# Key and strided-query loads in rows of 2 KB, and the first 64 tokens of all heads sorted by four ScalarE copies

## The chip, the core and the metric

The kernel runs on one core of a Trainium2 chip. Its time is the device time of one execution in microseconds (us); lower is better. TensorE (PE) does matmuls and transposes, VectorE (DVE), ScalarE (ACT) and GpSimd (POOL) do the elementwise work, and SyncE (SP) issues nearly every transfer, in the order of the program. 16 DMA engines move the data.

## The reference

The first half is attention with two kinds of heads over 8 batches, 8 heads, 576 tokens and 64 dimensions, and the second half is a soft mixture of experts over its output.

```python
scores = scale * np.matmul(q, k.transpose(0, 1, 3, 2))
rel = pos[:, None] - pos[None, :]
mask_local = (rel >= 0) & (rel < stride)                       # stride = 32
mask_strided = (rel >= 0) & (pos[None, :] % stride == pos[:, None] % stride)
masks = np.stack([mask_local if h < H // 2 else mask_strided for h in range(H)])
...                                   # softmax over the last axis, times v
x = attn_out.transpose(0, 2, 1, 3).reshape(B * S, H * D)       # 4608 x 512
logits = x @ phi                                               # 512 x 32
...                    # softmax over the tokens: d; softmax over the slots: c
slot_input = d.T @ x                                           # 8 experts x 4 slots
h = np.maximum(slot_input[e] @ w1[e], 0.0); slot_out[e] = h @ w2[e]
return c @ slot_out
```

So a token of a local head looks at the 32 last tokens, and one of a strided head at every 32nd token before it. Everything is in float32.

## The kernel before, in words

The attention runs in 16 steps, numbered i. Step i takes two local heads (called L) and two strided heads (called S) of batch i // 2. For tokens 64 to 575 it loads four arrays of 256 KB, `kL`, `qL`, `kS`, `qS` (`emit_D`, one transfer each, L306). For the first 64 tokens an even step loads a fifth array `t` with all eight heads of k and q, in two transfers of 128 KB (`emit_Dt`, L311). Values come in other transfers (L316 and L319 for local heads, L324 for strided heads, where each transfer has 36 rows of 4 KB), and between all of them a written-out list places loads of the experts' weights, 512 KB each (`w` in the list, L256).

In a load of L306 each of 128 partitions gets, for each of two heads, four consecutive tokens of 64 dimensions, so the memory is read in pieces of 1 KB. In the load of L311 each partition is one token, and the memory is read in pieces of 256 B, one for each head.

TensorE turns each loaded array over by four transposes of 128x128 into a bank of PSUM (`turn`, L340). ScalarE then copies the bank to SBUF and sorts it on the way: `kL` by four copies of 64 partitions by 256 elements (L356), `qL`, `qS` and `t` by one copy of 128 by 512 each (L350, L360, L375), `kS` by two copies (L364). From the copy of `t` (called `et`, into the last third of the tile `qtb`) GpSimd takes the keys of the first 64 tokens into the key tiles (`emit_kc`: L383, L387). Then come the scores (`emit_SL`, `emit_SS`, L390), a softmax on VectorE and ScalarE, and the products with the values (L470).

The order of all this work on every engine is set by one list that is written out by hand, `ORDER`. A name in it is a part and a step: `DkL.0` is the load of `kL` for step 0, `Tt.0` the transposes of `t`, `et.0` its copy. Each engine executes its instructions in the order of the list. The loads of one step go into a ring of four places in the tile `natb`, so a load also waits until an older one has been transposed.

After step 15 the sums over all tokens are merged, the first expert layer runs (L851), then the second (L963), and the results are combined and stored (L988, L996, L1010 to L1028).

Of the kernel before, what the change touches and what calls it, by code (L numbers as in the profile page):

```python
# [19 lines left out]
B, H, S, D = 8, 8, 576, 64  # L20
# [6 lines left out]
NI = 36  # L27
# [81 lines left out]
def tile_sparse_attention_soft_moe(  # L109
# [12 lines left out]
    nc = tc.nc  # L122
    P = 128
    ACT, DVE, PC = nc.scalar.copy, nc.vector.tensor_copy, nc.gpsimd.tensor_copy
# [6 lines left out]
    def big(nm, cols, dt=F32):  # L131
        return const.tile([P, cols], dt, name=nm)
# [10 lines left out]
    d = big("d", 128)  # L143
# [6 lines left out]
    kLb, kSb = big("kLb", 2 * S), big("kSb", 2 * S)  # L150
    qtb = big("qtb", 1536)
# [16 lines left out]
    def nat(x, i):  # L168
        if (x, i) in EARLY:
            lo = 512 * EARLY[x, i]  # L170
            return xnb[:, lo:lo + 512]
        lo = 512 * (USES.index((x, i)) % 4)
        return natb[:, lo:lo + 512]
# [6 lines left out]

    kL = kLb.rearrange("p (a t) -> p a t", a=2)
    kt = {"kL": kLb, "kS": kSb, "qL": qtb[:, 0:512], "qS": qtb[:, 512:1024]}
    tl = qtb[:, 1024:1536].rearrange("p (j x t) -> p j x t", j=4, x=2)

    psg = {1: pb[:, 0:640].rearrange("p (s k a) -> p s k a", s=5, a=2),
           2: pb[:, 640:1152].rearrange("p (s x) -> p s x", s=4)[:, :, 0:3 * NI].rearrange("p s (k a) -> p s k a", a=3)[:, :, :, 0:2]}
# [30 lines left out]
    def take():  # L217
        x = min(freed, key=lambda x: freed[x])
        del freed[x]
        return banks[x], x  # L220

    def give(t):
        clock[0] += 1
        freed[t[1]] = clock[0]
# [75 lines left out]
    def heads(i, s):  # L300
        h = 2 * (i % 2) + (4 if s == "S" else 0)
        return slice(h, h + 2)

    def emit_D(x, i):
        src = (k if x[0] == "k" else q)[i // 2, heads(i, x[1]), 64:]
        nc.sync.dma_start(out=nat(x, i).rearrange("p (h x) -> p h x", h=2), in_=src.rearrange("h (p n) d -> p h (n d)", n=TN))  # L306

    def emit_Dt(i):

        for x, src in enumerate((k, q)):  # L310
            nc.sync.dma_start(out=nat("t", i)[x::2].rearrange("t (h d) -> t h d", d=D), in_=src[i // 2, :, 0:64].rearrange("h t d -> t h d"))  # L311

    def emit_Dv(i):

# [32 lines left out]
    def emit_e(x, i):  # L347
        t = box.pop(("T" + x, i))
        if x == "qL":
            ACT(out=kt[x].rearrange("d (p n) -> d p n", n=TN), in_=t[0].rearrange("d (n p) -> d p n", n=TN))  # L350
        elif x == "kL":

            for a in range(2):
                dst = kL[64 * a:64 * a + 64, a, 64:]
                for n in range(2):
                    ACT(out=dst.rearrange("d (p j n) -> d p j n", j=2, n=2)[:, :, :, n],  # L356
                        in_=t[0][64 * n:64 * n + 64].rearrange("d (h j p) -> d p j h", j=2, h=2)[:, :, :, a])
        elif x == "qS":

            ACT(out=kt[x].rearrange("d (x m i) -> d x m i", m=4, i=32), in_=t[0].rearrange("d (x i m) -> d x m i", i=32, m=4))  # L360
        else:
            for n in range(2):
                r = slice(64 * n, 64 * n + 64)
                ACT(out=kt[x][r].rearrange("d (x m n i) -> d x m n i", m=4, n=2, i=NI)[:, :, :, n, 4:],  # L364
                    in_=t[0][r].rearrange("d (x i m) -> d x m i", i=32, m=4))
        give(t)
# [5 lines left out]

    def emit_et(i):
        t = box.pop(("Tt", i))
        ACT(out=tl, in_=t[0].rearrange("d (j t x) -> d j x t", j=4, x=2))  # L375
        give(t)

    def emit_kc(s, i):

        for a in range(2):  # L380
            h = slice(64 * a, 64 * a + 64)
            src = tl[h, i % 2 + (2 if s == "S" else 0), 0]
            PC(out=kL[h, a, 0:64] if s == "L" else kA[h, a], in_=src)  # L383
            if s == "S":
                for n in range(2):
                    dst = kSb[64 * n:64 * n + 64].rearrange("d (h j m x) -> d h j m x", h=2, m=4, x=2 * NI)[:, a, :, :, NI * n:NI * n + 4]
                    PC(out=dst, in_=src.rearrange("d (i m j n) -> d j m i n", i=4, m=4, n=2)[:, :, :, :, n])  # L387

    def score(t, c, x, wd, lhsT, rhs):
        nc.tensor.matmul(out=t[0][32 * c:32 * c + 32, x:x + wd], lhsT=lhsT, rhs=rhs, start=True, stop=True, skip_group_check=True)  # L390
# [8 lines left out]
    def emit_SS(i):  # L399
        t = box["M2", i] = take()  # L400
        for c in range(4):
            qa = tl[:, i % 2 + 2 * (c // 2), 1, 32 * (c % 2):32 * (c % 2) + 32]
            score(t, c, 0, 128, qa, kL[:, :, 0:64] if c < 2 else kA)
        for h in range(2):
            for z in range(2):
                for c in range(4):

                    x = 8 * h + 4 * z + c
                    score(t, c, 128 + 2 * NI * (2 * h + z), 2 * NI, kt["qS"][:, 32 * x:32 * x + 32], kSb[:, 2 * NI * x:2 * NI * x + 2 * NI])

    def part(t, which):
# [286 lines left out]
    for x in KQ:  # L698
        fns["D" + x] = lambda i, x=x: emit_D(x, i)
        fns["T" + x] = lambda i, x=x: emit_T(x, i)  # L700
        fns["e" + x] = lambda i, x=x: emit_e(x, i)
# [6 lines left out]
    for s in "LS":  # L708
        fns["kc" + s] = lambda i, s=s: emit_kc(s, i)
        fns["P" + s] = lambda i, s=s: emit_P(s, i)  # L710
        fns["f" + s] = lambda i, s=s: emit_f(s, i)
        fns["n" + s] = lambda i, s=s: emit_n(s, i)
        fns["X" + s] = lambda i, s=s: emit_X(s, i)
    fns.update(Dt=emit_Dt, Tt=emit_Tt, et=emit_et, Dv=emit_Dv, Ds=emit_Ds, C2=emit_C2, SL=emit_SL, SS=emit_SS, rc=emit_rc, PA=emit_PA,
               fA=emit_fA, AL=emit_AL, AS=emit_AS, AA=emit_AA, nA=emit_nA, xL=emit_xL, xS=emit_xS,
               XB=emit_XB, xB=emit_xB, LG=emit_LG, lc=emit_lc, lg=emit_lg, T9=emit_T9, x9=emit_x9, G9=emit_G9, c9=emit_c9, b9=emit_b9,
# [200 lines left out]
    for x in ORDER:  # L917
# [4 lines left out]
        else:  # L922
            n, i = x.split(".")
            i = int(i)
# [147 lines left out]
```

## Time and profile before

| | |
|---|---|
| median of 3 runs | 243.8 us (243.25 to 244.0) |
| the profiled execution, its own time | 242.59 us |
| its span from the first to the last instruction | 240.8 us |
| TensorE busy | 215.2 us, 89% of the span |
| VectorE busy | 165.6 us, 69% |
| ScalarE busy | 154.3 us, 64% |
| GpSimd busy | 86.0 us, 36% |
| moved by DMA | 72.73 MB, mean 302 GB/s |

The profiled execution took 1.8 us more than its span, and 1.2 us less than the median of the runs. A busy time is the time in which at least one instruction of the engine was under way; TensorE's matmuls overlap one another, so its share says little on how much more it could do. The share of DMA is the mean over 16 engines and can be a little over 1, since packets of one engine overlap.

### The profile page before, as it was taken

To read this page: it belongs to the slowest core of one execution; us is meant where nothing else is said; L and a number is where in the kernel's file an instruction comes from. 1 tells how busy PE (TensorE), PEld (TensorE's weight loads), DVE (VectorE), ACT (ScalarE), POOL (GpSimd) and SP (SyncE) were. 2 spreads that over 40 slices of the span, in tenths; PEclk is the share of its full clock that TensorE was granted. 3 is DMA by queue.
4 is the path that set the end of the run, shared out by engine and by line. 5 is a ranking of instruction groups with operands and counts; after the bars stand their busy time and mean duration, and the time that the engine had idled before them with its cause. 6 is when DMAs were issued, how large, how long until landed. Compare 5 with 4: busy or idle time off the path is not lost.

```text
span 240.8 us, 9926 instructions
## 1 busy us (share of the span) xinstructions
PE 215.2 (89%) x4096; PEld 169.0 (70%) x4096; DVE 165.6 (69%) x381; ACT 154.3 (64%) x347; POOL 86.0 (36%) x189
## 2 busy tenths in 40 slices
PE   8899998998889999999999999899889999998700
PEld 3688897888778998897889898687753246455400
DVE  6097997896599978887977786799872831145900
ACT  2789898786769889878697988666440241135700
POOL 5466835626443271743327434733102000000000
PEclk9999999999999999999999999999999999999975
DMA  5987999989997998899999899999998999887996
GB/s 151 351 231 238 301 282 279 302 207 318 304 321 218 299 317 236 263 344 297 318 367 340 233 280 335 316 284 358 349 344 338 395 377 312 293 287 257 381 399 260
DMA packets 69597, 72.73 MB, mean 302 GB/s; under 512 B 32896, under 2 KB 59664, under 8 KB 69552
## 3 DMA queue, kind: packets, MB, share of 16 engines
q1 hardware_dynamic: 69184, 71.84, 92.2%
q8 instruction: 32, 0.52, 0.9%
q0 software_dynamic: 80, 0.15, 0.2%
q10 hardware_dynamic: 288, 0.11, 0.2%
q14 instruction: 13, 0.11, 0.2%
HBM read 62.65 MB, written 9.44 MB: 299 GB/s over the span
## 4 chain that ended last, share of the span: by engine, by line
PE 54%; DMA 18%; DVE 13%; issue 4%; ACT 3%; POOL 2%; SPq 1%; DVEq 0%; POOLq 0%; ACTq 0%
PE bank L340 10%; PE bank L390 7%; PE bank L470 7%; DMA natb<-in_q_dram 6%; PE bank L851 6%; DMA vs<-in_v_dram 5%; PE bank L518 4%; DMA wb<-in_moe_w_dram 4%; PE bank L963 3%; PE bank L462 3%; PE bank L276 2%; PE bank L988 2%; DVE xnb L500 2%; DMA natb<-in_k_dram 2%; PE bank L549 2%
## 5 line engine op out<-in xcount | busy, mean ns | idle before, releaser
L340 PE MATMUL bank<-cf,natb 128*128 128x128 f32 x276 | 40.2, 277 | 3.0 <-DMA natb<-in_k_dram 1.3
L340 PEld LDWEIGHTS bank<-cf,natb 128*128 128x128 f32 x276 | 30.8, 141 | 8.0 <-issue 3.0
L356 ACT COPY kLb<-bank 64x256 f32<-64x256 f32 x64 | 25.8, 403 | 7.5 <-PE bank L340 4.7
L427 DVE TENSOR_TENSOR pb<-bank,cb 128x512 f32<-128x512 f32 (+2 forms) x48 | 21.7, 472 | 11.4 <-PE bank L390 7.4
L500 DVE TENSOR_TENSOR xnb<-bank,rz 128x512 f32<-128x512 f32 (+1 forms) x33 | 21.6, 669 | 7.6 <-PE bank L470 4.9
L330 POOL COPY vb<-vb 64x1024 f32<-64x1024 f32 x16 | 16.7, 1041 | 25.8 <-DMA vb<-in_v_dram 14.8
L390 PE MATMUL bank<-kLb,qtb 128*32 128x128 f32 x576 | 23.1, 274 | 0.8 <-POOL kLb L383 0.8
L442 DVE TENSOR_REDUCE rz<-pb 128x10 f32<-128x640 f32 (+1 forms) x32 | 21.6, 684 | 1.0 <-ACT pb L439 0.6
L466 ACT COPY ptb<-bank 128x512 f32<-128x512 f32 x32 | 19.0, 598 | 4.5 <-PE bank L462 2.9
L432 DVE TENSOR_REDUCE mx<-pb 128x10 f32<-128x640 f32 (+1 forms) x32 | 21.5, 685 | 0.5
L435 DVE TENSOR_TENSOR pb<-pb,mx 128x640 f32<-128x640 f32 (+1 forms) x32 | 21.1, 673 | 0.3
L439 ACT ACTIVATE pb<-pb 128x640 f32<-128x640 f32 (+1 forms) x32 | 18.6, 597 | 3.5 <-DVE pb L435 3.3
L335 POOL COPY natb<-natb 128x512 f32<-128x512 f32 x15 | 9.6, 638 | 30.1 <-DMA natb<-in_q_dram 18.9
L462 PE MATMUL bank<-cf,pb 128*128 128x128 f32 x128 | 19.4, 276 | 0.8 <-ACT d L619 0.7
L518 PE MATMUL bank<-cf,xnb 128*128 128x128 f32 x128 | 18.8, 277 | 0.7 <-DVE xnb L500 0.5
L390 PEld LDWEIGHTS bank<-kLb,qtb 128*32 128x32 f32 x576 | 17.1, 110 | 3.4 <-POOL kLb L383 1.5
L364 ACT COPY kSb<-bank 64x512 f32<-64x512 f32 x32 | 18.6, 581 | 0.4
L387 POOL COPY kSb<-qtb 64x32 f32<-64x32 f32 x64 | 17.5, 273 | 2.4
L470 PE MATMUL bank<-vs,ptb 128*32 128x128 f32 x480 | 16.0, 274 | 2.4 <-DMA vs<-in_v_dram 1.1
L470 PE MATMUL bank<-vb,ptb 128*32 128x128 f32 x512 | 17.4, 274 | 0.0
L331 POOL COPY vb<-vb 64x1024 f32<-64x1024 f32 x16 | 16.8, 1048 | 0.7
L518 PEld LDWEIGHTS bank<-cf,xnb 128*128 128x128 f32 x128 | 14.4, 141 | 2.6 <-issue 1.2
(199 smaller groups left out, 457.2 us busy)
## 6 DMA issues: line engine op xcount, KB each, us to landing
wb<-in_moe_w_dram SPq DMA_DIRECT2D x48, 512.0 KB
natb<-in_k_dram SPq DMA_DIRECT2D x30, 256.0 KB
natb<-in_q_dram SPq DMA_DIRECT2D x30, 256.0 KB
vb<-in_v_dram SPq DMA_DIRECT2D x32, 144.0 KB
vs<-in_v_dram SPq DMA_DIRECT2D x30, 144.0 KB
out_dram<-wb SPq DMA_DIRECT2D x16, 256.0 KB
vb<-in_moe_w_dram SPq DMA_DIRECT2D x4, 512.0 KB
xnb<-in_moe_w_dram SPq DMA_DIRECT2D x3, 512.0 KB
```

The source lines that it names most:

```text
L340: nc.tensor.transpose(out=t[0][:, 128 * n:128 * n + 128], in_=src[:, 128 * n:128 * n + 128], identity=ident)
L356: ACT(out=dst.rearrange("d (p j n) -> d p j n", j=2, n=2)[:, :, :, n], in_=t[0][64 * n:64 * n + 64].rearrange("d (h j p) -> d p j h", j=2, ...
L390: nc.tensor.matmul(out=t[0][32 * c:32 * c + 32, x:x + wd], lhsT=lhsT, rhs=rhs, start=True, stop=True, skip_group_check=True)
L427: nc.vector.tensor_tensor(out=dst, in0=src, in1=masks[w].unsqueeze(1).unsqueeze(3).to_broadcast([P, n, kk, 2]), op=ALU.add)
L432: nc.vector.tensor_reduce(out=part(box[i][0], w), in_=psg[w].rearrange("p s k a -> p s a k"), op=ALU.max, axis=AX.X)
L435: nc.vector.tensor_tensor(out=psg[w], in0=psg[w], in1=over(box[i][0], w), op=ALU.subtract)
L442: nc.vector.tensor_reduce(out=part(box[i][1], w), in_=psg[w].rearrange("p s k a -> p s a k"), op=ALU.add, axis=AX.X)
L462: nc.tensor.transpose(out=t[0][:, 128 * r:128 * r + 128], in_=pb[:, lo + 128 * r:lo + 128 * r + 128], identity=ident)
L466: ACT(out=ptL if s == "L" else ptS, in_=t[0])
L470: nc.tensor.matmul(out=t[0][32 * c:32 * c + 32, 128 * r:128 * r + 128], lhsT=lhsT, rhs=rhs, start=True, stop=True, skip_group_check=True)
L500: nc.vector.tensor_tensor(out=xn[:, place(i, s), r0:r0 + nr].rearrange("p r (a d) -> p r a d", a=2), in0=t[0][:, 128 * r0:128 * r0 + 128 * ...
L518: nc.tensor.transpose(out=t[0][:, 128 * r:128 * r + 128], in_=xn[:, place(i, s), r, :], identity=ident)
```

## The change

The loads of `kL`, `kS` and `qS` now give each partition eight consecutive tokens of one head, 2 KB in one piece. `qL` keeps its pieces of 1 KB. The load of `t` gives each of 64 partitions eight consecutive tokens of one head, again 2 KB in one piece, with k in partitions 0 to 63 and q in 64 to 127. After the transposes the tokens then stand in another order. For `kL` the four copies take another stride. For `t` the one copy of 128 by 512 becomes four copies of 64 by 256. The strided copies of GpSimd and the choice of columns in the strided scores follow the new order of tokens. `ORDER` stays as it is.

```diff
-    tl = qtb[:, 1024:1536].rearrange("p (j x t) -> p j x t", j=4, x=2)
+    tl = qtb[:, 1024:1536].rearrange("p (x j t) -> p j x t", j=4, x=2)
...
     def emit_D(x, i):
         src = (k if x[0] == "k" else q)[i // 2, heads(i, x[1]), 64:]
+        if x != "qL":
+            nc.sync.dma_start(out=nat(x, i), in_=src.rearrange("h (p n) d -> p h (n d)", n=8))
+            return
         nc.sync.dma_start(out=nat(x, i).rearrange("p (h x) -> p h x", h=2), in_=src.rearrange("h (p n) d -> p h (n d)", n=TN))
...
-            nc.sync.dma_start(out=nat("t", i)[x::2].rearrange("t (h d) -> t h d", d=D), in_=src[i // 2, :, 0:64].rearrange("h t d -> t h d"))
+            nc.sync.dma_start(out=nat("t", i)[64 * x:64 * x + 64], in_=src[i // 2, :, 0:64].rearrange("h (p n) d -> h p (n d)", n=8))
...
                 for n in range(2):
-                    ACT(out=dst.rearrange("d (p j n) -> d p j n", j=2, n=2)[:, :, :, n],
-                        in_=t[0][64 * n:64 * n + 64].rearrange("d (h j p) -> d p j h", j=2, h=2)[:, :, :, a])
+                    ACT(out=dst.rearrange("d (p b n) -> d p b n", b=4, n=2)[:, :, :, n],
+                        in_=t[0][64 * n:64 * n + 64].rearrange("d (b p h) -> d p b h", b=4, h=2)[:, :, :, a])
...
     def emit_et(i):
         t = box.pop(("Tt", i))
-        ACT(out=tl, in_=t[0].rearrange("d (j t x) -> d j x t", j=4, x=2))
+        for n in range(2):
+            for a in range(2):
+                ACT(out=qtb[64 * a:64 * a + 64, 1024:1536].rearrange("d (y p m n) -> d y p m n", p=8, m=4, n=2)[:, :, :, :, n],
+                    in_=t[0][64 * n:64 * n + 64].rearrange("d (m y a p) -> d y a p m", m=4, y=8, a=2)[:, :, a])
         give(t)
...
-                    x = 8 * h + 4 * z + c
+                    x = 4 * (2 * (c % 2) + z) + 2 * (c // 2) + h
```

On ScalarE, at the start of the program, the copies of the first step stand in this order before the change (a row is the line, the operation, the tile written and the bank read, the shape, and how many).

```order
L356 COPY kLb<-bank_118 64x256 x4
L375 COPY qtb<-bank_120 128x512
L350 COPY qtb<-bank_122 128x512
L364 COPY kSb<-bank_124 64x16x32 x2
L360 COPY qtb<-bank_119 128x512
L356 COPY kLb<-bank_121 64x256 x4
```

And so after it, where line numbers are higher by 3 to 6.

```order
L359 COPY kLb<-bank_118 64x256 x4
L380 COPY qtb<-bank_120 64x256 x4
L353 COPY qtb<-bank_122 128x512
L367 COPY kSb<-bank_124 64x16x32 x2
L363 COPY qtb<-bank_119 128x512
L359 COPY kLb<-bank_121 64x256 x4
```

Nothing has moved: in the place of the one copy of `t` (second row) stand four smaller ones, ahead of the same copy of `qL`. The other seven copies of `t` change in the same way.

On SyncE, at the start of the program, the first loads stand in this order before the change (the shape is that of the side in SBUF: partitions, pieces, elements of a piece).

```order
L306 DMA natb<-in_k_dram 128x2x256
L311 DMA natb<-in_k_dram 64x8x64
L311 DMA natb<-in_q_dram 64x8x64
L306 DMA natb<-in_q_dram 128x2x256
L306 DMA xnb<-in_k_dram 128x2x256
```

And so after it.

```order
L307 DMA natb<-in_k_dram 128x1x512
L314 DMA natb<-in_k_dram 64x1x512
L314 DMA natb<-in_q_dram 64x1x512
L309 DMA natb<-in_q_dram 128x2x256
L307 DMA xnb<-in_k_dram 128x1x512
```

Each load keeps its place; a piece is now 512 elements, except in the load of `qL` (fourth row).

## Rows read from the trace of the kernel before

**Rows 1.** The page: mean busy share of the DMA engines in 40 slices, tenths.

```profile
DMA  5987999989997998899999899999998999887996
```

**Rows 2.** Stretches: length; busy PE, PEld, DVE, ACT, POOL; clock; DMA share; GB/s.

```profile
0.00:150.00 150.00, 142.27 (x2994) 124.52 (x2995) 117.72 (x261) 120.97 (x272) 74.17 (x172) 1.00 0.94 285
150.00:206.00 56.00, 52.94 (x817) 32.24 (x815) 35.60 (x98) 22.69 (x54) 11.81 (x17) 1.00 0.97 339
```

**Rows 3.** The chain that ended last: shares of the span by engine.

```profile
PE 54%; DMA 18%; DVE 13%; issue 4%; ACT 3%; POOL 2%; SPq 1%; DVEq 0%; POOLq 0%; ACTq 0%
```

**Rows 4.** The page: packets, MB and share of 16 engines of SyncE's DMA queue.

```profile
q1 hardware_dynamic: 69184, 71.84, 92.2%
```

**Rows 5.** DMA of 12.5 to 14.5 us, where nearly all packets have 256 B.

```profile
DMA packets 1750, 0.45 MB, mean 223 GB/s; under 512 B 1748, under 2 KB 1749, under 8 KB 1749
...
q1 hardware_dynamic: 1749, 0.43, 95.9%
```

**Rows 6.** DMA of 212 to 218 us, where packets of 1 KB are stored.

```profile
DMA packets 2176, 2.10 MB, mean 350 GB/s; under 512 B 128, under 2 KB 2176, under 8 KB 2176
...
q1 hardware_dynamic: 2176, 2.10, 99.7%
```

**Rows 7.** DMA of 202 to 206 us, where packets of 1 KB are loaded.

```profile
DMA packets 1116, 1.12 MB, mean 281 GB/s; under 512 B 35, under 2 KB 1115, under 8 KB 1115
...
q1 hardware_dynamic: 1115, 1.11, 100.9%
```

**Rows 8.** DMA of 233 to 237 us, where packets of 2 KB are stored.

```profile
DMA packets 886, 1.62 MB, mean 405 GB/s; under 512 B 96, under 2 KB 96, under 8 KB 886
...
q1 hardware_dynamic: 886, 1.62, 105.0%
```

**Rows 9.** ScalarE from 18.8 us: start, us, line, operation, shapes, count, idle before.

```profile
18.86 0.62 ACT L375 COPY qtb<-bank 128x512 f32<-128x512 f32 x1
19.33 0.63 ACT L466 COPY ptb<-bank 128x512 f32<-128x512 f32 x1
19.81 1.69 ACT L356 COPY kLb<-bank 64x256 f32<-64x256 f32 x4
```

**Rows 10.** The first step: ScalarE, GpSimd and TensorE behind the first copy of `t`.

```profile
8.39 0.59 ACT L375 COPY qtb<-bank 128x512 f32<-128x512 f32 x1
...
9.04 0.23 POOL L383 COPY vb<-qtb 64x64 f32<-64x64 f32 x1 [1.23 <-ACT qtb L375]
...
11.13 1.08 PE L390 MATMUL bank<-kLb,qtb 128*32 128x128 f32 x32 [0.65 <-POOL kLb L383]
```

**Rows 11.** ScalarE behind the copy of `t` at 96 us, with an idle time.

```profile
96.18 0.59 ACT L375 COPY qtb<-bank 128x512 f32<-128x512 f32 x1
...
98.16 0.59 ACT L360 COPY qtb<-bank 128x512 f32<-128x512 f32 x1 [0.66 <-PE bank L340]
```

**Rows 12.** SyncE's issues by line: shortest, median and longest ns, first and last start.

```profile
L306 SPq DMA_DIRECT2D natb<-in_q_dram x30: 367/419/1396, 2.7 to 143.6; - x30
...
L311 SPq DMA_DIRECT2D natb<-in_k_dram x8: 602/637/740, 1.2 to 134.8; - x8
...
L319 SPq DMA_DIRECT2D vb<-in_v_dram x16: 602/622/1930, 10.0 to 150.3; - x16
...
L324 SPq DMA_DIRECT2D vs<-in_v_dram x30: 758/792/902, 15.9 to 153.2; - x30
```

**Rows 13.** SyncE from 66.5 us: start, us, line, transfer, count.

```profile
66.58 1.62 SPq L324 DMA_DIRECT2D vs<-in_v_dram  x2
...
72.06 0.60 SPq L311 DMA_DIRECT2D natb<-in_k_dram  x1
...
74.10 1.84 SPq L306 DMA_DIRECT2D natb<-in_k_dram  x1
```

**Rows 14.** The DMA share in two stretches beside rows 13, columns as in rows 2.

```profile
72.00:74.00 2.00, 2.00 (x68) 1.66 (x63) 1.91 (x6) 1.98 (x5) 0.00 (x0) 1.00 0.74 177
...
76.00:78.00 2.00, 2.00 (x19) 1.82 (x17) 1.90 (x3) 1.60 (x5) 0.62 (x1) 1.00 0.72 231
```

More of the change, by code (lines that the diff above doesn't have):

```diff
@@ L385, in emit_kc @@
                 for n in range(2):
-                    dst = kSb[64 * n:64 * n + 64].rearrange("d (h j m x) -> d h j m x", h=2, m=4, x=2 * NI)[:, a, :, :, NI * n:NI * n + 4]
-                    PC(out=dst, in_=src.rearrange("d (i m j n) -> d j m i n", i=4, m=4, n=2)[:, :, :, :, n])
+                    dst = kSb[64 * n:64 * n + 64].rearrange("d (b m h x) -> d h b m x", h=2, m=2, x=2 * NI)[:, a, :, :, NI * n:NI * n + 4]
+                    PC(out=dst, in_=src.rearrange("d (i m b n) -> d b m i n", i=4, m=2, n=2)[:, :, :, :, n])
     def score(t, c, x, wd, lhsT, rhs):
```

## The prediction, made before the changed kernel ran

> **What bounds the kernel now.** I read the stretches first. Up to 150 us, where all the changed loads and copies lie, the 16 DMA engines are busy 0.94 of the time, and ScalarE 121.0 of 150 us, 81% [rows 2]. From 150 to 206 us the DMA share is 0.97, but almost all of that is expert weights, which the change doesn't touch. The slices show that the DMA engines are not full throughout: 8 of the first 25 (6 us each) lie under nine tenths [rows 1]. The chain of work that ended last says the same in another way: 54% TensorE, 18% DMA, 13% VectorE, only 3% ScalarE [rows 3]. So no engine bounds this kernel alone. The transfers come nearest to it; ScalarE runs close behind with little idle time, and a step that comes late on it is not late for long as a rule.
>
> The idle of the DMA engines is read beside SyncE. From 66.6 us to beyond 75 us SyncE issues with hardly a gap [rows 13], yet the DMA share is 0.74 and 0.72 in two stretches of 2 us there [rows 14]. There the issuing, or a wait inside it, and not the moving, sets the pace.
>
> **The change, part by part.**
>
> *Packet times.* I take stretches in which one packet size rules, and divide engine time by packets. For 256 B: 0.959 x 16 x 2 us / 1749 = 17.5 ns [rows 5]. For 1 KB stored: 0.997 x 16 x 6 us / 2048 = 46.7 ns [rows 6]; for 1 KB loaded, 202 to 206 us, 1.009 x 16 x 4 us / 1080 = 59.8 ns [rows 7]. For 2 KB only stores exist: 1.05 x 16 x 4 us / 790 = 85 ns [rows 8]. The small packets that signal the end of a transfer are left out of the last three, which makes them slightly high.
>
> *`kL`, `kS`, `qS`.* 48 loads had 256 packets of 1 KB, so 12288 / 16 = 768 on each engine; now it is 384 of 2 KB, 384 x 85 ns = 32.6 us. Before, 768 packets cost 35.9 us at 46.7 ns or 45.9 us at 59.8 ns. The gain is 3.3 us for each engine at the low price, 13.3 us at the high one. I take 3.3: the high price comes from a stretch in which weights arrive beside other traffic at 281 GB/s, and I can't tell whether 2 KB loads would escape what slowed it.
>
> *`t`.* 16 loads had 512 packets of 256 B: 512 on each engine, 9.0 us. Now there are 1024 packets of 2 KB in all. Spread over 16 engines, that is 64 x 85 ns = 5.4 us, a gain of 3.6. But are they spread? SyncE's queue has 69184 packets [rows 4]. From the program 65152 carry data: 28672 of 256 B, 26624 of 1 KB, 1536 of 2 KB, 8320 of 4 KB. The other 4032 are end signals; 260 transfers at 16 each would be 4160, so 128 are missing, which is 4 for each of the 32 loads of L324. These have 36 rows, and every other transfer has 64 or 128 on its outer side. So a load of 36 rows runs on 12 engines, the largest number up to 16 that divides 36. The new load of `t` has the 8 heads as the outer dimension in memory, and by the same pattern runs on 8 engines. These then carry 128 packets, 10.9 us, 1.9 more than now; the others carry none and are relieved by 9.0. Only the transfers that use all engines wait for the fullest ones, and the fullest are the 8. The Trainium skill, page "DMA: Bandwidth & Descriptors", section "Why a DMA increments its semaphore by 16 and not by 1", gives this as a rule: the engines used are the largest number up to 16 that divides the outer sizes of both sides. By that rule `t` goes to 8 engines, and the trace agrees with it for 36 rows.
>
> So the DMA term lies between -1.4 us on the 8 fullest engines (3.3 less, 1.9 more) and -6.9 us if all share `t`. I take -1.4.
>
> *The copies of `t`.* One copy keeps ScalarE for 0.47 us (the next starts that much later), four of 64 x 256 for 1.69 us [rows 9]: 1.2 us more, eight times. At the start it is on the path: GpSimd waits for this copy, and TensorE's first scores wait for GpSimd [rows 10]. Four copies end 1.69 us after 8.39 us and not 0.59 us after it, so everything behind moves by 1.1 us. Of the other seven, 8.4 us together, the cost lies between nothing and all. The copy at 18.9 us stands in solid work [rows 9]; behind the one at 96 us ScalarE idles 0.66 us within 2 us [rows 11], which takes up half of it. I take 2.0 us: one in full, and a little over a tenth of the other six, since ScalarE is only 3% of the chain. Behind a late copy stand the copies of `qL`, of `kS` and the exponentials, and for these TensorE and VectorE wait.
>
> *Issuing.* A load of L306 keeps SyncE for about 0.42 us. Loads whose outer side is 64 take 0.61 to 0.64, the one on 12 engines 0.79 [rows 12]. In memory the new loads have 64 outside and 2 heads inside, so their issue lies between 0.42 and 0.64 us, and that of `t` between 0.64 and 0.79: at most 48 x 0.2 + 16 x 0.15 = 12.0 us of SyncE's time. At the other end stands a gain, since single issues of up to 1.4 to 1.9 us [rows 12, 13] look held up by what was queued before them, and fewer packets are queued now. I take nothing.
>
> *Nothing.* The copies of `kL`, the transposes, GpSimd's copies and the scores keep their number and sizes; only strides change. The copies of ScalarE in [rows 9] take 0.62, 0.63 and 4 x 0.42 us with quite different strides, so I count no difference.
>
> **The sum**, from the profiled execution: 242.6 + 1.1 + 2.0 - 1.4 = 244.3 us. That execution lies 1.2 us under the median of the runs, so against the median it is 243.8 + 1.7 = **245.5 us**.
>
> **The rivals.**
>
> *The relief counts in full, faster.* If `t` is spread over all engines, or if the mean load and not the fullest engines set the pace, the DMA term is -6.9 us: 243.8 + 3.1 - 6.9 = **240.0 us**. For it speaks that loads are a large part of the chain (18% DMA), against it the missing end signals and the slices in which the engines are not full. It decides once the relief is over the 3.1 us that ScalarE costs. At the high price of 1 KB loads it would go well below that, to about 230 us; I give this little.
>
> *SyncE becomes the bound, slower.* If the issues grow by the full 12.0 us and this counts in the 8 of 25 slices in which the DMA engines are not full, it is 3.8 us; the DMA term counts in the other 17 only, -1.0: 243.8 + 3.1 + 3.8 - 1.0 = **249.7 us**. For it speak rows 13 and 14, against it the held-up issues, which could take it up.
>
> *No difference.* Later copies are absorbed, the first 1.1 us too, because the loads set the pace later anyway: 243.8 + 1.1 - 1.4 = **243.5 us**.
>
> That packets would not become larger can be set aside: stores of 2 KB already run as 2 KB packets [rows 8].
>
> **Chances and range.** The forecast (245.5, its own range 244.6 to 248) gets 0.42, the full relief 0.33, SyncE 0.13, no difference 0.12. A measurement here tells about 0.3% from no change, 0.7 us. Of the forecast 0.03 lies within that. Faster: 0.33. Within 0.3%: 0.12 + 0.03 = 0.15. Slower: 0.39 + 0.13 = 0.52. The range reaches from just under the full relief to SyncE's case, 239.5 to 250.0 us, and leaves out some of both ends, 2 in 10.
>
> **What the changed profile would show.** SyncE's queue has 69184 - 6144 - 7168 = 55872 packets, less 128 more, 55744, if `t` runs on 8 engines; this alone settles that step. The DMA share up to 150 us falls to about 0.90 while the loads land no sooner. ScalarE is busy some 8 us longer up to 150 us, the first scores start at about 12.2 us, not 11.1. If the issue of the new loads takes 0.6 us or more and SyncE has no gaps, its rival is right. I am wrong if the loads wait clearly less for one another in the middle of the kernel, so that the last scores start earlier despite a later start.

## The result, and the profile after

The changed kernel takes 245.74 us (median of 20 runs) against 243.13 us before (20 runs). The ratio is 1.014, with a 95% interval of 1.010 to 1.018: it is slower, by about 3.4 us. This ratio, and every one below, leaves out the runs that lie more than 1.5% above the fastest of their kernel, while the medians are over all runs and differ by 2.6 us.

The page after is read at SyncE's queue first; before, it had 69184 packets [rows 4].

```profile
q1 hardware_dynamic: 55744, 71.84, 90.5%
```

55744 is what was worked out for `t` on 8 engines, to the packet; 16 engines would make 55872. So the packets did become larger. The time that they took, as a share of 16 engines' span, fell from 92.2% to 90.5%, but of a span that is 2.7 us longer: from 222.0 to 220.4 us on each engine, 1.6 us, where the packet times had promised 6.9 us on the mean. The first experiment comes back to this.

The chain that ended last, by engine and then by line, shows where the loss came in.

```profile
PE 50%; DVE 21%; ACT 11%; DMA 7%; issue 5%; POOL 1%; DVEq 0%; ACTq 0%; POOLq 0%
PE bank L396 8%; PE bank L343 7%; PE bank L476 6%; PE bank L857 5%; DMA wb<-in_moe_w_dram 4%; DVE xnb L506 4%; PE bank L524 3%; PE bank L969 3%; ACT qtb L380 3%; PE bank L468 3%; DVE pb L433 2%; DVE rz L448 2%; PE bank L276 2%; PE bank L994 2%; DVE mx L438 2%
```

Transfers went from 18% of the chain to 7%, ScalarE from 3% to 11%, VectorE from 13% to 21% [rows 3]. On this chain there is less waiting for loads than before, and more for ScalarE's copies out of PSUM and for VectorE. The line L380, the new copies of `t`, alone holds 3%. A chain is that of one execution, but this sign is steady: in the five kernels, here and below, that copy `t` by four copies on ScalarE at least seven times of the eight, ScalarE has 10% to 13% of the chain, and in the kernels that always copy it by one, 1% to 5%. It is a sign and not a price, for `t` alone below has 10% as well and is only 0.4% slower than before.

The first stretch of [rows 2], with the same columns, shows how far that went.

```profile
0.00:150.00 150.00, 141.18 (x2937) 121.28 (x2941) 115.63 (x257) 125.97 (x287) 71.98 (x171) 1.00 0.91 282
```

ScalarE's busy time up to 150 us rose by 5.0 us, to 84% of the stretch, though less of the program lies in it now (2937 matmuls against 2994). Over the whole span it rose from 154.3 to 162.6 us, 8.3 us, which is the some 8 us that the copies were expected to cost ScalarE. The DMA share fell from 0.94 to 0.91. The last of the scores that read `kLb` start at 160.1 us, against 157.4 before: the sign of being wrong that the prediction named, last scores that start earlier, did not come, and the loss is there in full at that point.

The start after the change, on ScalarE, GpSimd and TensorE, answers to [rows 10] row by row.

```profile
8.84 1.60 ACT L380 COPY qtb<-bank 64x256 f32<-64x256 f32 x4
...
10.10 0.23 POOL L389 COPY vb<-qtb 64x64 f32<-64x64 f32 x1 [1.86 <-ACT qtb L380]
...
12.19 1.08 PE L396 MATMUL bank<-kLb,qtb 128*32 128x128 f32 x32 [1.28 <-POOL kLb L389]
```

The four copies take 1.60 us, GpSimd waits for them 1.86 us and not 1.23, and the first scores start at 12.19 us, 1.06 us later. But of this 1.06 us the copies made only 0.61. They began at 8.84 us and the one copy before at 8.39, so 0.45 us was lost ahead of them. From the start of the copying to the first scores it is 3.35 us, where it was 2.74, since GpSimd begins at 10.10 us, when three of the four copies are through (the third ends at 10.04 us), and not when all are. The second copy of `t` stands, as before, in work without a gap.

```profile
19.91 1.64 ACT L380 COPY qtb<-bank 64x256 f32<-64x256 f32 x4
21.57 0.59 ACT L472 COPY ptb<-bank 128x512 f32<-128x512 f32 x1
```

The queue is held for 1.66 us here (to 21.57 us), where it was 0.47 us [rows 9]. Who waited for the copies of `t` in the whole kernel (us, times), first before and then after:

```profile
  POOL kLb L383: 8.8, 2
  POOL vb L383: 6.5, 2
  PEld bank L549: 0.2, 1
```

```profile
  POOL kLb L389: 10.9, 5
  POOL vb L389: 1.9, 1
  PEld bank L343: 0.8, 2
  PEld bank L555: 0.7, 1
  PE bank L476: 0.5, 1
  PE bank L555: 0.4, 1
  PE bank L343: 0.4, 1
```

GpSimd waits longest, since it makes the keys from these copies, but no longer in all than before, 12.8 us against 15.3. What is new is that TensorE waits for them: six times where it was once, at transposes and products that have nothing to do with `t`. For the transposes the code names the reason: `turn` takes a bank, and `emit_et` gives one back only when its copies are through. SyncE's issues after, shortest, median and longest in ns, answer to [rows 12].

```profile
L307 SPq DMA_DIRECT2D natb<-in_k_dram x30: 535/592/1182, 0.7 to 144.9; - x30
...
L314 SPq DMA_DIRECT2D natb<-in_k_dram x8: 629/641/744, 1.5 to 135.2; - x8
L314 SPq DMA_DIRECT2D natb<-in_q_dram x8: 607/620/859, 2.3 to 136.1; - x8
```

A load of `kL` or `kS` takes SyncE 0.59 us to issue, 0.54 us at the shortest; a load of L306 took 0.42 us, 0.37 at the shortest [rows 12]. The loads of `t`, with an eighth of the packets, on half of the engines, take as long as before.

### The profile page after: what moved, and what is told of

It is laid out like the page before. It is cut to its first block, busy times and chain, and to the rows that moved or that the text cites. A ratio compares the mean times of both kernels' runs of the same rounds, so it can differ in the third digit from the quotient of the medians.

```text
span 243.5 us, 9959 instructions
## 1 busy us (share of the span) xinstructions
PE 217.2 (89%) x4096; PEld 168.9 (69%) x4096; DVE 166.2 (68%) x381; ACT 162.6 (67%) x371; POOL 84.6 (35%) x189
## 3 DMA queue, kind: packets, MB, share of 16 engines
q1 hardware_dynamic: 55744, 71.84, 90.5%
## 4 chain that ended last, share of the span: by engine, by line
PE 50%; DVE 21%; ACT 11%; DMA 7%; issue 5%; POOL 1%; DVEq 0%; ACTq 0%; POOLq 0%
PE bank L396 8%; PE bank L343 7%; PE bank L476 6%; PE bank L857 5%; DMA wb<-in_moe_w_dram 4%; DVE xnb L506 4%; PE bank L524 3%; PE bank L969 3%; ACT qtb L380 3%; PE bank L468 3%; DVE pb L433 2%; DVE rz L448 2%; PE bank L276 2%; PE bank L994 2%; DVE mx L438 2%
## 5 line engine op out<-in xcount | busy, mean ns | idle before, releaser
L445 ACT ACTIVATE pb<-pb 128x640 f32<-128x640 f32 (+1 forms) x32 | 18.8, 599 | 2.5 <-DVE pb L441 2.3
L393 POOL COPY kSb<-qtb 64x32 f32<-64x32 f32 x64 | 15.7, 245 | 2.5
L468 PEld LDWEIGHTS bank<-cf,pb 128*128 128x128 f32 x128 | 14.5, 141 | 2.7 <-ACT pb L445 1.0
```

The lines of the kernel that those rows point to most:

```text
L468: nc.tensor.transpose(out=t[0][:, 128 * r:128 * r + 128], in_=pb[:, lo + 128 * r:lo + 128 * r + 128], identity=ident)
```

## The experiments

All ratios are to the kernel before. 1% is 2.4 us. The theories that the experiments set against each other: the four copies on ScalarE make the loss (1); the dearer issue on SyncE does (2); `t` on 8 engines holds up all loads (3).

**One copy in place of four.**

```diff
 def emit_et(i):
-    for n in range(2):
-        for a in range(2):
-            ACT(out=qtb[64 * a:64 * a + 64, 1024:1536]..., in_=t[0][64 * n:64 * n + 64]...)
+    ACT(out=qtb[:, 1024:1536].rearrange("d (y p m) -> d y p m", p=16, m=4),
+        in_=t[0].rearrange("d (m y p) -> d y p m", m=4, y=8))
```

> The changed kernel, but the copy of t is one instruction of 128 by 512 again, as before the change; the first 64 tokens are left unsorted, so the scores of these tokens mix tokens. ScalarE theory (the four copies cost 1.1 us at the start and 1 to 2 us later, and are what makes the change slower): the first scores start at about 11.1 us, and the ratio to before falls from 1.014 to 0.995 to 1.002. SyncE theory (the new loads take 0.55 to 0.6 us to issue and not 0.42, some 9 us in all): the ratio stays at 1.008 to 1.014. Theory of the eight engines (t on 8 of 16 engines makes all loads land late): it stays at 1.008 or more too.

Measured: 1.000 (0.996 to 1.005). The loss is gone with the copies. The first scores are back near their old place, 2.74 us behind the start of the copy, as before the change.

```profile
8.30 0.59 ACT L378 COPY qtb<-bank 128x512 f32<-128x512 f32 x1
...
11.04 1.18 PE L393 MATMUL bank<-kLb,qtb 128*32 128x128 f32 x34 [0.95 <-POOL kLb L386]
```

The chain of this kernel gives ScalarE its old small share, and the transfers theirs:

```profile
PE 56%; DMA 16%; DVE 14%; issue 3%; POOL 2%; ACT 2%; SPq 1%; DVEq 0%; ACTq 0%; POOLq 0%
```

So theory 1 holds: the four copies cost 1.4%, 3.4 us, and the intervals of the two kernels lie apart. What this run leaves is as notable: with larger packets in `kL`, `kS`, `qS` and `t` and no extra copy, the kernel is no faster than before.

The packets of this run show how little transfer time was gained.

```profile
q1 hardware_dynamic: 55744, 71.84, 92.1%
```

That is 92.1% of 240.9 us, 221.9 us on each engine, against 222.0 before: of the 6.9 us almost nothing was saved. The price of a load can be read in two stretches in which one size rules, 16 to 18 us in the kernel before and 17 to 19 us in the changed one.

```profile
DMA packets 557, 0.54 MB, mean 268 GB/s; under 512 B 35, under 2 KB 557, under 8 KB 557
q1 hardware_dynamic: 557, 0.54, 84.1%
...
DMA packets 275, 0.51 MB, mean 254 GB/s; under 512 B 29, under 2 KB 29, under 8 KB 275
q1 hardware_dynamic: 275, 0.51, 79.0%
```

By the prediction's way of reckoning this is 0.841 x 16 x 2 us / 522 = 51.6 ns for a loaded packet of 1 KB, and 0.790 x 16 x 2 us / 246 = 102.8 ns for one of 2 KB. Over all packets of 1 KB before and of 2 KB after, up to 150 us, the means are 51.7 and 101.9 ns. So on the mean twice the bytes took twice the time, and the 48 loads of `kL`, `kS` and `qS` took 39.1 us on each engine after 39.7 before. The typical packet was as the prediction priced it from stores, 46 and 84 ns at the median; the means are higher because some packets took several times as long. Why those did is not shown.

**The two parts apart.** The first takes `emit_Dt`, `emit_et` and the view `tl` of the change, and the rest from before; the second takes the opposite parts.

> Only the part on t: its load in pieces of 2 KB on 8 engines and the four copies; kL, kS and qS as before. ScalarE theory: 1.010 to 1.018, the whole loss without the gain of the larger packets of the keys. SyncE theory: the issue of t takes as long as before (0.62 to 0.64 us), so about 1.000 to 1.004. Theory of the eight engines: 1.010 or more.

Measured: 1.004 (1.001 to 1.008).

> Only the part on kL, kS and qS: pieces of 2 KB; t as before, in pieces of 256 B on 16 engines with one copy. ScalarE theory: no loss is left, 0.985 to 1.000, by the 3.3 us of packet time at most. SyncE theory: the loss stays, 1.006 to 1.015. Theory of the eight engines: 0.985 to 1.000 as well.

Measured: 1.003 (0.998 to 1.008); the median of all its runs was 0.9% above that of before. Neither part alone is as slow as both, and neither is faster. `t` alone came out below what theory 1 expected, which is a miss of that theory's size. The keys alone came out at or above it: something beside ScalarE may cost in the keys' part, but the interval holds no change as well. The two parts add up to 0.7%, and both together cost 1.4%; the intervals leave that difference open.

**`t` on 16 engines.**

```diff
-in_=src[i // 2, :, 0:64].rearrange("h (p n) d -> h p (n d)", n=8)
+in_=src[i // 2, 0, 0:512].rearrange("(p n) d -> p (n d)", n=8)
```

> The changed kernel, but t is read from 64 rows of 2 KB that lie one behind the other in memory, so that its outer size is 64 and it runs on 16 engines; the bytes are other tokens, so the first 64 tokens of the output are not attention. SyncE's queue should have 55872 packets and not 55744. ScalarE theory: 1.008 to 1.014, little change. Theory of the eight engines: the lower eight engines lose 5.5 us of 10.9, and the ratio falls to 0.99 to 1.004. SyncE theory: 1.008 to 1.014.

Measured: 1.008 (1.004 to 1.012). The queue's row shows 16 engines; but the issue of `t` became cheaper as well, 0.55 and 0.59 us at the median, where it was 0.64 and 0.62:

```profile
q1 hardware_dynamic: 55872, 71.84, 91.6%
...
L314 SPq DMA_DIRECT2D natb<-in_k_dram x8: 518/550/1377, 1.5 to 135.1; - x8
L314 SPq DMA_DIRECT2D natb<-in_q_dram x8: 588/593/602, 2.1 to 135.7; - x8
```

By the prediction's packet times the 8 fullest engines lost 5.5 us of work. The kernel gained 1.5 us at the middle of the intervals, which overlap, so that a gain is not shown. Theory 3, in which the fullest engines set the pace, expected 0.99 to 1.004, and the interval only just reaches there. The first experiment speaks against it more clearly: one copy, with `t` still on 8 engines, took the whole loss away, where theory 3 expected 1.008 or more.

**The first copy alone.** `emit_et(0)` is one copy as above, the other seven are four each.

> The changed kernel, but the very first copy of t is one instruction of 128 by 512 and the other seven are four each; the first 64 tokens of batch 0 are left unsorted. If the start counts in full, the first scores start at 11.1 us and the ratio falls from 1.014 by 1.1 us, to 1.007 to 1.011. If the start is absorbed later, it stays at 1.012 to 1.016. If the start is nearly all of ScalarE's cost, it falls to 1.000 to 1.005.

Measured: 1.008 (1.002 to 1.013). Its first scores start early, but its copy of `t` does too; between the two lie 2.75 us, as with one copy everywhere:

```profile
8.06 0.59 ACT L379 COPY qtb<-bank 128x512 f32<-128x512 f32 x1
...
10.81 1.18 PE L400 MATMUL bank<-kLb,qtb 128*32 128x128 f32 x34 [0.71 <-POOL kLb L393]
```

At the middle of the intervals the first of the eight copies makes about half of the loss: 1.6 us from 1.014 to 1.008, and the other seven 1.8 us, from there to 1.000. But this interval overlaps that of the changed kernel and that of one copy, so the split is not shown, nor that a delay at the start is never made up: the expected case in which it is absorbed, 1.012 to 1.016, is not ruled out.

**Two of the four copies on VectorE.**

```diff
-                ACT(out=qtb[64 * a:64 * a + 64, 1024:1536]...
+                (ACT, DVE)[n](out=qtb[64 * a:64 * a + 64, 1024:1536]...
```

> The changed kernel with two of the four copies of t on VectorE and two on ScalarE; it computes the reference. If the time of ScalarE's queue is what makes the change slower, half of it is gone: 1.002 to 1.010. If VectorE, which is 77% busy up to 150 us and carries 21% of the chain after the change, is as tight: 1.010 to 1.020.

Measured: 1.023 (1.018 to 1.029), above both ranges at its middle, and worse than all four on ScalarE, if only just clear of it. The profile, of the longest of the six runs, shows a wait that the edit brought in: VectorE stood idle before its two copies until ScalarE's two were through (us, times).

```profile
  ACT qtb L380: 9.7, 6
```

A copy of `t` took 0.43 us on VectorE and 0.39 on ScalarE, so the two shares ran one behind the other, and from the start of the copying to the first scores it was 3.41 us, no less than with all four on ScalarE. That VectorE has less room than ScalarE, with 78% busy up to 150 us against 81% [rows 2], is therefore not shown by this run.

**The keys' part with a cheap issue.** The rows of 2 KB lie one behind the other in memory, 128 outside on both sides.

```diff
-nc.sync.dma_start(out=nat(x, i), in_=src.rearrange("h (p n) d -> p h (n d)", n=8))
+flat = (k if x[0] == "k" else q)[i // 2].rearrange("h t d -> (h t) d")
+lo = 64 + 576 * heads(i, x[1]).start
+nc.sync.dma_start(out=nat(x, i), in_=flat[lo:lo + 1024].rearrange("(p n) d -> p (n d)", n=8))
```

> The keys' part alone as in the run before, but kL, kS and qS are read from 128 rows of 2 KB that lie one behind the other, so that both sides have 128 outside; the second head's tokens are shifted, so the output is not attention. Packets, bytes and engines are those of the keys' part alone. Theory that the dear issue eats what the larger packets give: the issue falls from 0.60 to about 0.42 us, and the ratio from 1.003 to 0.985 to 0.997. Theory that the larger packets give nothing, since the loads' packet time is not what is waited for: 1.000 to 1.006 as without the cheap issue.

Measured: 0.983 (0.975 to 0.991). This rests on the two lowest of only six times; the median of all six, 241.5 us, is 0.7% under that of before. Not its size but at most its sign is to be carried on, and two more kernels ask again: the same edit on the changed kernel, with four copies, and with one copy as well.

> The changed kernel with its four copies, only the issue of the keys cheap (the second head's tokens shifted). If the dear issue costs 1% or more: 0.998 to 1.006 in place of 1.014. If ScalarE's copies alone make the loss: 1.010 to 1.016.

Measured: 1.010 (1.004 to 1.017), at the edge of what was expected if ScalarE's copies alone make the loss. Its four copies of the first step and its first scores lie as follows.

```profile
7.70 1.60 ACT L382 COPY qtb<-bank 64x256 f32<-64x256 f32 x4
...
11.03 1.18 PE L398 MATMUL bank<-kLb,qtb 128*32 128x128 f32 x34 [0.79 <-POOL kLb L391]
```

From the one to the other it is 3.33 us, as after the change, and yet the scores start at 11.03 us, earlier than in the kernel before (11.13): a single start time says less than this distance.

> The changed kernel with both suspected costs off: t in one copy of 128 by 512 (left unsorted) and the cheap issue of the keys (the second head's tokens shifted). Only the larger packets and the eight engines for t are left. ScalarE and SyncE theory together: 0.975 to 0.992, 1% or more below the kernel with one copy alone (1.000). If the issue costs nothing: 0.997 to 1.003.

Measured: 0.993 (0.988 to 0.997), between the two ranges. It lies apart from the 1.010 of the same kernel with four copies, so these cost 1.8%, 4.3 us, here: the second pair of kernels in which their cost is clear of the noise. The issue in the kernel with four copies is cheap indeed, 0.42 and 0.35 us at the median:

```profile
L309 SPq DMA_DIRECT2D natb<-in_k_dram x30: 327/416/1230, 0.7 to 141.9; - x30
L309 SPq DMA_DIRECT2D natb<-in_q_dram x15: 327/349/1470, 6.0 to 140.2; - x15
```

With four copies the cheap issue gives 0.4%, with one copy 0.8% (1.000 to 0.993), with the keys alone 2.0%. The intervals of the first two pairs overlap, and those of the third lie apart but rest on two times. All three have the same sign, so a second, smaller cost, between 0.9 and 1.9 us in the first two pairs, is likely and not shown. The issue need not be its cause: reading from one stretch and not from two heads is part of this edit, and was not separated from it.

**`t` alone with one copy.** The part on `t` as above, with the one copy of the first experiment.

> The part on t alone, pieces of 2 KB on 8 engines, but with one copy of 128 by 512; the first 64 tokens are left unsorted. It shows what the load of t gives by itself. ScalarE theory: 0.992 to 1.000, so that the four copies cost 0.5% to 1% here too (the part with four copies stood at 1.004). Theory of the eight engines, which by the packet times would cost the fullest ones 1.9 us: 1.002 to 1.008.

Measured: 0.984 (0.977 to 0.990), again on the two lowest of six times, so it was run once more.

> The part on t with one copy once more, since its ratio of 0.984 rested on two low times of six. If the load of t in 2 KB gives 1% or more by itself: 0.980 to 0.992. If those two were chance: 0.995 to 1.002, and then the four copies cost 0.4% to 0.9% there.

Measured: 0.997 (0.992 to 1.002), on twelve times. The larger packets of `t` by themselves, on 8 engines, lie between a gain of 2.0 us and a cost of 0.4 us; theory 3 expected a cost of 0.2% to 0.8%, and the interval ends where that begins. Against the part with four copies (1.004) the copies cost 0.8% here at the middle, and the intervals overlap a little.

**Sorting on TensorE.** The part on `t` alone, one copy of 128 by 512, and matmuls that write each head to its half of the partitions.

```diff
-        turn("Tt", i, nat("t", i))
+        for n in range(8):
+            for a in range(2):
+                nc.tensor.matmul(out=t[0][64 * a:64 * a + 64, 64 * n:64 * n + 64], lhsT=src[:, 64 * n:64 * n + 64],
+                                 rhs=ident.rearrange("k (y a p) -> k a y p", a=2, p=8)[:, a], ...)
```

> It computes the reference. The part on t alone (pieces of 2 KB on 8 engines; keys as before), but sorted by TensorE: 16 matmuls of 64 columns against chosen columns of the identity write each head to its half of the partitions, in place of four transposes, and one copy of 128 by 512 follows. ScalarE theory: the cost of the four copies is gone and TensorE's 12 more matmuls for each t hide under other work: 0.990 to 1.000, below the 1.004 of the part with four copies. If TensorE has no room, 1.003 or more.

Measured: 1.015 (1.006 to 1.024), from the lowest three of six times. Its TensorE rows at the start show the price: the columns are start, us, line, operation, shape and count.

```profile
6.05 0.60 PE L340 MATMUL bank<-cf,natb 128*128 128x128 f32 x4
6.49 0.38 PE L282 MATMUL bank<-wb 128*128 128x512 bf16 x1
7.57 1.15 PE L373 MATMUL bank<-cf,natb 128*64 128x64 f32 x32 [0.70 <-DMA natb<-in_q_dram]
8.65 0.39 PE L282 MATMUL bank<-wb 128*128 128x512 bf16 x1
```

Four transposes hold TensorE 0.44 us (6.05 to 6.49), the 16 matmuls, recorded as 32, hold it 1.08 us. That is 0.64 us more eight times, 5.1 us, and the kernel lost 1.8%, 4.4 us, against the one copy without this sorting (0.997). I had expected TensorE to hide it; it didn't. The copy that follows sorts otherwise than that of the other kernel, so that the cost lies in the matmuls is likely and not separated. None of the kernels that keep the whole computation is faster than the kernel before.

## Why the prediction was right, point by point

The forecast was slower, 245.5 us against 243.8, by 1.7 us; measured is slower by 3.4 us at the ratio and 2.6 us at the medians. The sign was right, and so was the main mechanism: ScalarE's four copies are what makes the change slower, and the larger packets don't pay for them. The loss was larger. That 245.74 us came out beside the forecast 245.5 is partly luck, since the kernel before lies at 243.13 over 20 runs and not at 243.8: a starting point too high and a loss too small cancel. Term by term:

*All copies of `t`* (1.1 + 2.0 = 3.1 us): right. Taking them away gives 3.4 us, and 4.3 us with the cheap issue, both clear of the noise; with `t` alone it is 1.8 us at the middle. That ScalarE had only 3% of the chain before was no reason for nothing: after the change it has 11%.

*The first copy* (1.1 us): the path is right, the step to the scores is not. GpSimd starts behind the third of the four copies, so that the scores move by 0.6 us and not by 1.1; that they start 1.06 us later, at the 12.2 us that was forecast, is luck, since 0.45 us of it lay ahead of the copies. The run without it is 1.6 us faster at the middle, with overlapping intervals. The copies of `qL` and `kS` behind it in ScalarE's queue do wait for all four.

*The other seven copies* (2.0 us): 1.8 us at the middle by the two runs that enclose it, which overlap too.

*The larger packets* (-1.4 us): -1.8 us in the run with both costs off, 0.7 to 3.0 by its interval. So the number came near, but neither of its reasons holds. The prices of 85 and 46.7 ns were taken from stores; the loads took 101.9 and 51.7 ns on the mean, and their engines' time fell by 0.1 us with one copy and, with both costs off, by 0.4 us (91.8% of 241.4 us), not by 6.9 us on the mean; in the changed kernel itself it was 1.6 us. And that the 8 fullest engines set the pace is not borne out: that `t` runs on 8 engines is shown by the packets, but 16 engines gave 1.5 us at the middle and not 5.5, and `t` alone with one copy on 8 engines was not slower. What made the 1.8 us is open.

*Issuing* (nothing): this is the term that was most likely mis-sized. The bounds of 0.42 to 0.64 us held for the keys, at 0.59 us at the median; `t`, at 0.64 and 0.62 us, stayed at the lower end of its bounds or just under it. (The rows give 0.62 to 0.64 us, and not 0.61, for loads with 64 outside.) I let the held-up issues take it up, and they did in part: added up over the traces, the loads of `kL`, `qL`, `kS`, `qS` and `t` kept SyncE 48.1 us before and 50.5 us after, with the longest single issue at 1.84 and 1.40 us. One trace is a weak measure of this, for in `t` alone, where the keys are loaded as before, it was 41.2 us. The two runs with the cheap issue in the changed kernel, in which it was 40.7 us, are 0.9 and 1.9 us faster than their partners, within overlapping intervals. By the kernels with one copy the change is 1.6 + 1.8 us for the copies, 1.9 us for the issue and 1.8 us less for the rest, 3.5 us in all. This is no proof of the parts, for they are differences of the same runs and must add up to the measured loss.

*The rivals.* The full relief (240.0 us) did not come: with both costs off the gain was 1.8 us, 3.0 at most, and not 6.9, and the transfers were hardly relieved at all. SyncE as the bound (249.7 us) did not come: the issue took nearly the 0.6 us of its sign, but one copy alone took the whole loss away with the dear issue in place. No difference (243.5 us) is ruled out by the interval of the result.

## What to carry to other kernels

Where several engines are busy 78% or more in a written-out order, as the DMA engines, TensorE, ScalarE and VectorE are here up to 150 us, work put on one of them can cost a good part of itself, whatever its share of the chain: 8.3 us more for ScalarE cost 3.4 and 4.3 us in the two pairs of kernels that are clear of the noise. Count what a new layout of a load asks of the engines that must undo it before counting what it saves in transfers. Take the price of a packet from loads of the same kind and at their mean, and look at whether the engines' total time falls. And larger packets are not a cheaper transfer to issue when the two sides of the load no longer have the same outer shape: look at the row of the issue. To read what a copy delays, measure from its own start, not from the start of the program.

## What the runs showed of the hardware that I had not expected

A load of 128 pieces of 2 KB takes SyncE 0.55 to 0.59 us to issue when memory is walked as 64 by 2 and SBUF as 128, and 0.35 to 0.42 us when both are walked as 128; the larger number of pieces before, 256, took 0.42 to 0.45 us (medians by line and array). So in these loads the shape counts, not the number of pieces.

A load of 2 KB pieces took its engines as long as the same bytes in pieces of 1 KB: 101.9 against 2 x 51.7 ns on the mean, though 84 against 2 x 46 ns at the median.

A matmul in float32 against a part of the identity is recorded twice, a transpose of the same data once: 16 matmuls of 64 columns held TensorE for 1.08 us and four transposes of 128 columns for 0.44 us, though both move the same 128 by 512 elements.
